# A state-space convolution with a SwiGLU layer: the powers of the large lag factor from TensorE and PSUM

## The chip, the core and the metric

The kernel runs on one core of a Trainium2 chip. The core has five engines that each work off a queue of their own in order: TensorE (PE in the profile; its weight loads are shown apart as PEld), VectorE (DVE), ScalarE (ACT), GpSimd (POOL) and SyncE (SP), which here only issues DMAs. They wait for each other by semaphores. The metric is the device time of one execution in microseconds.

## What is computed

Two layers, each a state-space convolution with a residual, followed by a SwiGLU feed-forward part with a residual, over 2048 positions of 512 channels. Both layers use the same parameters, so the filter K is formed once. Cut to what matters:

```python
def _A_ref(u, A_re, A_im, B_re, B_im, C_re, C_im, log_dt, Dskip):
    dt = jnp.exp(log_dt)[:, None]
    logdA = dt * (A_re + 1j * A_im)                        # [512, 128]
    dB = dt * (B_re + 1j * B_im)
    P = jnp.exp(logdA[:, :, None] * l[None, None, :])      # l = 0 .. 2047
    K = jnp.einsum("dn,dnl,dn->dl", C_re + 1j * C_im, P, dB).real
    y = irfft(rfft(u, 2 * L) * rfft(K, 2 * L))[:L]         # per channel
    return y + u * Dskip

def _B_ref(x, w_gate, w_up, w_down):
    return (silu(x @ w_gate) * (x @ w_up)) @ w_down

x = A_u
for _ in range(2):
    x = x + _A_ref(layernorm(x), ...)
    x = x + _B_ref(layernorm(x), ...)
```

## The kernel before

The first 290 us form the filter. The 512 channels go in eight chunks of 64 channels; the 128 states lie on the partitions. A lag is split as l = 32 a + z, with a from 0 to 63 and z from 0 to 31. For each chunk the kernel forms a large factor, the powers exp(32 a r) times a sine or cosine (tiles `re` and `im`, 64 channels by 65 values of a), and a small factor `g` with the weights in it (64 channels by 32 values of z). `r` is the real rate `rho` = dt A_re. For each channel TensorE multiplies both over the states (`lags`, 128 products of 32 by 64 into the PSUM tile `pk`). ScalarE copies `pk` out (`ks`, L476), TensorE spreads it (`spread`, `kp`), ScalarE copies that (`kt`, L947), and `spectra` turns it into the filter's spectrum with matrices of cosines, for four residues q in turn: products `pw` (L507), a copy by ScalarE (L516), sums by GpSimd (L518 to L528), and stores of `wdr` by SP.

The magnitudes of the large factor are formed by `gen_exp`, on ScalarE alone. `mz` holds six small powers (L393). `re[:, :, a]` for a from 1 to 32 and `mu[:, :, a - 32]` for a from 33 to 63 hold exp(32 a r): an exponential of 128x64 (L398) for each odd a and each a that divides by 8, and the others as squares of those at half the exponent (L401). That makes 39 exponentials and 4 squarings for a chunk.

The three engines ACT, DVE and PE have an order written out by hand in this stage (`manual_schedule`); the rows of SP and GpSimd, and all that follows the stage, are placed by a scheduler. The hand-written order is a loop of seven turns over i:

- `lags(i)`, the rest of the third and the whole fourth spectrum of chunk i-1, `spread_in` (the copy `ks`)
- on VectorE the small factor of chunk i+1 (`gen_g`) and its large one (`gen_e`), and the phases of chunk i+2 (`gen_turns`, `gen_reduce`)
- on ScalarE the sines of chunk i+2 (`gen_trig`), then `kt`, then `gen_exp` of chunk i+2, whose pieces `take(ex, n)` are laid between copies of spectra and other work
- two times in a turn `norm_units(3, 9)`: three tiles of the feed-forward weights are loaded (`st`), squared by ScalarE (`sq`, L309), and multiplied by ones on TensorE (`nrm`, L313), for bounds on the weights' norms. The second half of this, `norm_units(0, 0)`, gives the products to TensorE. In the second one of a turn they stand between the second and the third spectrum, so TensorE's queue stops there until the squares are done.
- one unit of `second`, a part of the input's forward transform (`pf`, L279)

[...] Two tiles of two banks each (tag `big`) serve `pk` and `kp` by turns; four tiles of one bank (tag `sml`) serve the spectra, the norms and `pf`.

The feed-forward stage from about 300 us on takes most of the time and is one long run of fp16 products on TensorE.

Of the kernel before, what the change touches and what calls it, by code (L numbers as in the profile page):

```python
# [22 lines left out]
P = 128  # L23
# [4 lines left out]
HD = D // 2  # L28
# [6 lines left out]
DC = 64  # L35
NCH = D // DC
ZP = (1, 2, 3, 4, 8, 16)
NZ = len(ZP)
NA = NZ + 16
# [7 lines left out]
def dft_constants():  # L47


    j = np.arange(P)[:, None]  # L50
    r = np.arange(P)[None, :]
    ef = np.zeros((P, 4, 3, P), np.float64)
    ei = np.zeros((P, 4, 3, P), np.float64)
    ek = np.zeros((P, 4, 3, 2, P), np.float64)
    for q in range(4):
        f = q + 8 * r + 0.5
        e = np.exp(-2j * np.pi * ((j * f) / 1024.0))
        ef[:, q, 0], ef[:, q, 1], ef[:, q, 2] = e.real, e.imag, -e.real
        et = e.T / 512.0
        ei[:, q, 0], ei[:, q, 1], ei[:, q, 2] = et.real, et.imag, -et.imag  # L60
        for c in range(1, 4):
            ec = np.exp(-2j * np.pi * (((j + P * c) * f) / 1024.0))
            ek[:, q, c - 1, 0], ek[:, q, c - 1, 1] = ec.real, ec.imag
    am = np.zeros((P, NA), np.float64)
    am[:, :NZ] = ZP
    am[:, NZ:] = 32.0 * np.arange(17, 33)
    halves = []
    for e in (ef * 256.0, ei * 8192.0):
        hi = e.astype(np.float16)
        halves.append(np.stack([hi, (e - hi).astype(np.float16)], 3))  # L70
    return [a.astype(np.float32) for a in (ef, ei, ek, am)] + halves
# [3 lines left out]
def kernel(ctx, tc, x, a_re, a_im, b_re, b_im, c_re, c_im, log_dt, d_skip,  # L75
                           w_gate, w_up, w_down, c_ef, c_ei, c_ek, c_am, c_eh, c_eih, out):
    nc = tc.nc
    V, A, G, PE = nc.vector, nc.scalar, nc.gpsimd, nc.tensor
# [29 lines left out]
    nc.sync.dma_start(am, c_am)  # L108
    xne = tl([P, 2, 4, D], "xne", "gb")
    xe, ne = xne[:, 0], xne[:, 1]  # L110
    for c in range(0, 4, 2):
# [18 lines left out]
    wx = sb.tile([P, D], F16, name="wx")  # L130
# [203 lines left out]

    mz2 = tl([P, 2, NZ, DC], "mz2", "y1")
    tmp = btl[:, :4 * HD].rearrange("p (i s d) -> p i s d", i=2, s=8), tl([P, 16, DC], "tmp", "t")

    def gen_tiles(ch):  # L340
# [47 lines left out]
    def gen_exp(ch, ts):  # L388

        re, im, mu, xz, mz, t16 = ts  # L390
        r_ = rho[:, ch * DC:(ch + 1) * DC]
        for lv, m in enumerate(ZP):
            A.activation(mz[:, lv], r_, AF.Exp, scale=float(m))  # L393
            yield
        G.memset(re[:, :, 0], 1.0)
        for a0, o in ((0, re), (32, mu)):
            for a in [a for a in range(a0 + 1, a0 + 33) if a < 64 and (a % 2 or a % 8 == 0)]:
                A.activation(o[:, :, a - a0], r_, AF.Exp, scale=32.0 * a)  # L398
                yield
            for st in (2, 4):  # L400
                A.activation(o[:, :, st:33:2 * st] if a0 == 0 else o[:, :, st::2 * st],  # L401
                             re[:, :, (a0 + st) // 2:(a0 + 34) // 2:st], AF.Square)
                yield

    def gen_e(ts):
# [57 lines left out]
    def lags(ts, g):  # L463
        re, im = ts[:2]
        pk = pbig([P, 16, 64], "pk")
        for d in range(DC):
            grp, dd = d % 4, d // 4
            d = 16 * grp + dd
            o = pk[32 * grp:32 * grp + 32, dd, :]
            PE.matmul(o, lhsT=g[:, 0, :, d], rhs=re[:, d, 0:64], start=True, stop=False, tile_position=(0, 32 * grp))  # L470
            PE.matmul(o, lhsT=g[:, 1, :, d], rhs=im[:, d, 0:64], start=False, stop=True, tile_position=(0, 32 * grp))
        return pk

    def spread_in(pk):
        ks = tl([P, 4, 16, 16], "ks", "nn")
        A.activation(ks, pk.rearrange("p d (c a) -> p a c d", a=4), AF.Copy)  # L476
        return ks
# [78 lines left out]
    def take(it, n):  # L556
        for _ in range(n):
            next(it, None)
# [287 lines left out]
    ts = [None] * (NCH + 2)  # L846
# [13 lines left out]
    with tc.manual_schedule(engines={mybir.EngineType.Activation, mybir.EngineType.DVE, mybir.EngineType.PE}):  # L860
        ts[0], ts[1] = gen_tiles(0), gen_tiles(1)
        ex = gen_exp(0, ts[0])
# [42 lines left out]
        ex = gen_exp(1, ts[1])  # L905
# [2 lines left out]
        take(ex, 13)  # L908
        take(fw[7], 1)
        kt2 = tl([P, 2, 4, 16, 16], "kt2", "xf")  # L910
        sec = [(h, q) for h in range(2) for q in QORD]
        sp = iter(())
        for i in range(NCH - 1):
            pk = lags(ts[i], gs[i])
            more = i + 2 < NCH
            tn = rd = f = iter(())
            if more:
                ts[i + 2] = gen_tiles(i + 2)
                tn = gen_turns(i + 2, ts[i + 2])
            gs[i + 1] = tl([P, 2, 32, DC], "g", ("gb", "ga")[i % 2])  # L920
            gg, ge = gen_g(i + 1, ts[i + 1], gs[i + 1]), gen_e(ts[i + 1])
            take(ex, 100)
            take(sp, 2)
            norm_units(3, 9)
            norm_units(0, 0)
            ks = spread_in(pk)
            for g in (gg, tn, gg, tn):
                take(g, 1)
            if more:
                rd = gen_reduce(ts[i + 2])  # L930
                next(rd)
            for g in (gg, gg, ge, gg, ge, gg, gg, rd, rd, ge, rd, rd, ge, rd, rd, rd, rd):
                take(g, 1)
            while tops:
                tops.pop(0)()
            take(sp, 1)
            take(gg, 2)
            kp = spread(i, ks)
            if more:
                f = second(*sec[i])  # L940
                next(f)
            take(gg, 2)
            if more:
                tr = gen_trig(ts[i + 2])
                take(tr, 1)
            kt = kt2[:, i % 2]
            A.activation(kt, kp, AF.Copy)  # L947
            take(tr, 1)
            take(f, 1)
            take(tr, 1)  # L950
            if more:
                sp = spectra(i, kt, 0, NB)
                take(sp, 1)
                ex = gen_exp(i + 2, ts[i + 2])
                take(ex, 10)
                norm_units(3, 9)
                take(ex, 4)
                take(sp, 2)
                norm_units(0, 0)
                take(ex, 14)  # L960
                take(sp, 2)
                sizes(i, kt, ks)
                take(ge, 4)
                take(gg, 1)
                while tops:
                    tops.pop(0)()
                ts[i] = gs[i] = None
            else:
                sizes(i, kt, ks)
                take(ge, 4)  # L970
                take(gg, 1)
# [19 lines left out]
        i = NCH - 1  # L991
# [99 lines left out]
```

## Time and profile before

| what | value |
|---|---|
| median of three runs | 1200.64 us (1198.14 to 1202.4) |
| the profiled execution | 1200.92 us, its span 1199.1 us |
| PE busy, share of the span | 1102.7 us, 92% |
| PEld | 857.4 us, 72% |
| DVE | 1022.5 us, 85% |
| ACT | 650.4 us, 54% |
| POOL | 176.4 us, 15% |

Shares over the whole span say little about the stage that is changed. In the page's forty slices of 30 us, ACT has a 9 or an 8 in the tenths place from the second to the ninth slice, that is up to 270 us, and then falls off; DVE and PE are busy in most slices. What follows is read from windows and timelines of that stage. In a row of a timeline stand the start and the length in microseconds, the engine, the line, the operation, what it writes and reads, the shapes, how many instructions the row joins, and in brackets the idle time ahead of it and what ended it. Rows that join many instructions give the time that they took together.

### The profile page before, as it was taken

How to read it: one execution, taken by the hardware profiler on the slowest of the kernel's cores; microseconds unless marked ns; L12 is line 12 of the kernel's file. 1: busy time of each engine (PE TensorE's matmuls, PEld its weight loads, DVE VectorE, ACT ScalarE, POOL GpSimd, SP SyncE). 2: the span in 40 equal slices, each digit the busy share in tenths (PEclk: the TensorE clock that was granted, in tenths of full speed). 3: DMA queues.
4: the chain of work that ended last, by engine and by line, in shares of the span. 5: the costliest groups of instructions: out<-in, count | busy, mean ns of one | idle time of the engine just before them, and what ended most of it. 6: DMA issues, size and time to landing. Idle time of an engine off the chain costs nothing.

```text
span 1199.1 us, 25374 instructions
## 1 busy us (share of the span) xinstructions
PE 1102.7 (92%) x10220; PEld 857.4 (72%) x10220; DVE 1022.5 (85%) x1621; ACT 650.4 (54%) x1400; POOL 176.4 (15%) x225
## 2 busy tenths in 40 slices
PE   2978998988988989999999999999999989999998
PEld 2846776766875767778777686868687776867875
DVE  7988999996979998999999999999993899983211
ACT  6999999982256544636654533745432552224111
POOL 1104355542310010001100100110000010000000
PEclk9979899989999999999999999999999999999999
DMA  6444455558389428332344354334434144311000
GB/s 228 124 110 116 108 124 117 124 149 238 113 288 238 127 71 205 126 120 89 93 135 135 115 163 143 111 96 138 142 125 137 45 106 131 122 53 45 15 24 18
DMA packets 137161, 147.05 MB, mean 123 GB/s; under 512 B 76177, under 2 KB 85393, under 8 KB 137042
## 3 DMA queue, kind: packets, MB, share of 16 engines
q1 hardware_dynamic: 132178, 128.64, 35.8%
q0 software_dynamic: 4864, 16.78, 5.9%
q8 instruction: 80, 1.31, 0.5%
q14 instruction: 39, 0.32, 0.1%
HBM read 98.71 MB, written 28.31 MB: 106 GB/s over the span
## 4 chain that ended last, share of the span: by engine, by line
PE 46%; DVE 17%; issue 4%; DMA 3%; ACT 2%; POOL 1%; SPq 1%; DVEq 0%; ACTq 0%; POOLq 0%
PE pgu L821 8%; PE pgu L822 8%; PE pgu L823 8%; PE py L835 5%; PE py L837 5%; PE py L836 5%; PE pi L716 4%; PE pf L263 4%; DVE t L697 2%; DVE yk L700 2%; DVE yk L697 2%; DVE z L219 2%; DMA mix<-nn 1%; DVE sg L827 1%; DVE bt L219 1%
## 5 line engine op out<-in xcount | busy, mean ns | idle before, releaser
L821 PE MATMUL pgu<-mix,wsl 128*128 128x256 f16 x1280 | 349.8, 273 | 5.6 <-DVE sg L827 4.1
L823 PE MATMUL pgu<-mix,wsl 128*128 128x256 f16 x1280 | 349.7, 273 | 1.5 <-DVE wsl L593 1.5
L822 PE MATMUL pgu<-mix,wsl 128*128 128x256 f16 x1280 | 349.8, 273 | 0.0
L835 PE MATMUL py<-wsl,hh 128*128 128x512 f16 (+1 forms) x352 | 134.5, 382 | 11.0 <-DVE xg L840 4.9
L822 PEld LDWEIGHTS <-wsl 128*128 128x128 f16 x1280 | 125.5, 98 | 22.3 <-issue 6.6
L823 PEld LDWEIGHTS <-wsl 128*128 128x128 f16 x1280 | 125.6, 98 | 16.7 <-DVE wsl L593 1.8
L837 PE MATMUL py<-wsl,hl 128*128 128x512 f16 (+1 forms) x352 | 134.8, 383 | 2.7 <-DVE hl L829 2.7
L821 PEld LDWEIGHTS <-wsl 128*128 128x128 f16 x1280 | 125.6, 98 | 16.0 <-issue 0.3
L697 DVE TENSOR_TENSOR t<-uu,w 128x1024 f32<-128x1024 f32 x96 | 117.4, 1223 | 5.9 <-DMA uu<-udr 5.6
L836 PE MATMUL py<-wsl,hh 128*128 128x512 f16 x320 | 122.3, 382 | 0.0
L826 ACT ACTIVATE sg<-pgu,sc 128x512 f32<-128x512 f32 x80 | 54.5, 681 | 117.5 <-PE pgu L823 99.7
L700 DVE TENSOR_TENSOR yk<-yk,t 128x1024 f32<-128x1024 f32 x96 | 117.4, 1222 | 0.1
L827 DVE SCALAR_TENSOR_TENSOR sg<-pgu,sc,sg 128x512 f32<-128x512 f32 x80 | 60.0, 750 | 49.6 <-ACT sg L826 49.5
L507 PE MATMUL pw<-kt,ek 128*128 128x256 f32 (+2 forms) x420 | 102.0, 382 | 0.0
L716 PE MATMUL pi<-yl,mix 128*128 128x256 f16 x672 | 91.7, 273 | 6.3 <-ACT yl L705 4.4
L828 ACT ACTIVATE hh<-sg 128x512 f16<-128x512 f32 x80 | 50.1, 626 | 78.0 <-DVE sg L827 77.9
L507 PEld LDWEIGHTS pw<-kt,ek 128*128 128x128 f32 x420 | 81.5, 202 | 10.9
L263 PE MATMUL pf<-z,eh 128*128 128x256 f16 x576 | 75.8, 273 | 0.0
L716 PEld LDWEIGHTS <-mix 128*128 128x128 f16 x672 | 65.2, 98 | 12.3 <-issue 2.2
L705 ACT ACTIVATE yl<-mix,sy 128x512 f16<-128x512 f32 x56 | 40.2, 718 | 61.1 <-DVE mix L702 60.7
L214 POOL TENSOR_TENSOR rs<-mv,mhalf 128x2 f32<-128x2 f32 (+1 forms) x21 | 35.2, 1675 | 246.7 <-ACT mv L213 246.7
L836 PEld LDWEIGHTS <-hh 128*128 128x128 f16 (+1 forms) x352 | 34.7, 99 | 48.4 <-issue 13.5
(231 smaller groups left out, 2285.0 us busy)
## 6 DMA issues: line engine op xcount, KB each, us to landing
w<-wdr SPq DMA_DIRECT2D x96, 256.0 KB, 2.7
uu<-udr SPq DMA_DIRECT2D x96, 256.0 KB, 3.0
udr<-u POOLq DMA_DIRECT2D x32, 256.0 KB, 2.4
wdr<-wo SPq DMA_DIRECT2D x96, 64.0 KB, 2.4
udr<-u SPq DMA_DIRECT2D x16, 256.0 KB, 2.8
g<-tmp POOLq DMA_DIRECT2D x8, 512.0 KB, 4.6
g<-btl POOLq DMA_DIRECT2D x8, 512.0 KB, 5.9
n<-ndr SPq DMA_DIRECT2D x16, 256.0 KB, 3.0
```

The costliest lines, as they stand in the source:

```text
L263: PE.matmul(pf[:, o], lhsT=e, rhs=m, start=k == 0, stop=k == len(terms) - 1)
L507: PE.matmul(pw[:, i], lhsT=e, rhs=kt[:, :, c + 4 * k0:4 * k1:4, :].rearrange("p g k d -> p k g d"), start=c == 0, stop=c == 3)
L697: V.tensor_tensor(t, uu.unsqueeze(1).to_broadcast([P, 2, 2, HD]), w.unsqueeze(2).to_broadcast([P, 2, 2, HD]), OP.mult)
L700: V.tensor_tensor(yk, yk, t, OP.add)
L716: PE.matmul(pi[:, o], lhsT=e, rhs=m, start=k == 0, stop=k == len(terms) - 1)
L821: PE.matmul(o, lhsT=wgu(wi, k, 0)[:, fs], rhs=nh[:, k], start=k == 0, stop=False)
L822: PE.matmul(o, lhsT=wgu(wi, k, 0)[:, fs], rhs=nlo[:, k], start=False, stop=False)
L823: PE.matmul(o, lhsT=wgu(wi, k, 1)[:, fs], rhs=nh[:, k], start=False, stop=k == 3)
L827: V.scalar_tensor_tensor(sg, pgu[:, 1], sc6[:, 4:5], sg, OP.mult, OP.mult)
L835: PE.matmul(py[:, r], lhsT=hh[:n, f, rc], rhs=wd(f, 0)[:n], start=f == 0, stop=False)
L836: PE.matmul(py[:, r], lhsT=hh[:n, f, rc], rhs=wd(f, 1)[:n], start=False, stop=False)
L837: PE.matmul(py[:, r], lhsT=hl[:n, f, rc], rhs=wd(f, 0)[:n], start=False, stop=f == FT - 1)
```

## The change

From the third chunk on (chunk 2) `gen_exp` returns after the six small powers. The exponents 32 a r of the large factor are then formed by TensorE. GpSimd splits the rates of two chunks into three bf16 parts that add up to the fp32 value (`parts`). A DMA transpose (`turned`) turns each chunk's parts, so that 112 partitions hold, for two groups of 16 channels, the parts by channel, with the states along the free axis (`lts`). A constant table holds the multiples 32 a in blocks, zero elsewhere. It is appended to the constant `c_am`, bf16 values packed in pairs as fp32 words, and loaded once into the second half of `kt2` (`tab`). A product of both gives 16 channels by 32 exponents in one bank; two of them fill a tile `pm` of the `big` tag, and one exponential of 128x32x32 reads it and writes a half of `re` or `mu` (`gen_mags`). A chunk takes four such steps: eight products of 512 columns and four exponentials. `kt` now uses one buffer for all chunks. The place for the parts is in the tile of `mz`, the remainders are kept in `wx`, which is used later for weights, and `lts` in the last part of `btl`.

```diff
+    tab = np.zeros((2, 4, 16, 2, 2, 16, 32), np.float32)
+    for e in range(2):
+        for d in range(16):
+            tab[e, :3, d, 0, e, d] = 32.0 * np.arange(1, 33)
+            tab[e, :3, d, 1, e, d] = 32.0 * np.arange(33, 65)
+    tab = (tab.reshape(P, -1).view(np.uint32) >> 16).astype(np.uint16).view(np.float32)
+    am = np.concatenate([am.astype(np.float32), tab], 1)
...
-    mz2 = tl([P, 2, NZ, DC], "mz2", "y1")
+    mzp = tl([P, 4 * HD], "mzp", "y1")
+    mz2 = mzp[:, :2 * NZ * DC].rearrange("p (c l d) -> p c l d", c=2, l=NZ)
+    pt = mzp[:, 3 * HD:].bitcast(BF16).rearrange("p (c g q d) -> p c g q d", c=2, g=4, q=4)
+    r1 = wx.bitcast(F32)[:, :2 * DC].rearrange("p (c g d) -> p c g d", c=2, g=4)
+    lts = btl[:, 6 * HD:].bitcast(BF16).rearrange("p (c g n) -> p c g n", c=2, g=2)
+    G.memset(pt, 0.0)
...
         G.memset(re[:, :, 0], 1.0)
+        if ch > 1:
+            return
...
+    def parts(ch):
+        src = rho[:, ch * DC:(ch + 2) * DC].rearrange("p (c g d) -> p c g d", c=2, d=16)
+        hi, mid, lo = (pt[:, :, :, q] for q in range(3))
+        G.tensor_copy(hi, src)
+        G.tensor_tensor(r1, src, hi, OP.subtract)
+        G.tensor_copy(mid, r1)
+        G.tensor_tensor(lo, r1, mid, OP.subtract)
+
+    def turned():
+        for c in range(2):
+            nc.sync.dma_start_transpose(lts[:, c], pt[:, c].rearrange("p g q d -> p (g q d)"))
+
+    def gen_mags(ch, ts):
+        for k, o in enumerate((ts[0][:, :, 1:33], ts[2][:, :, 1:])):
+            for h in range(2):
+                pm = pbig([P, 32, 32], "pm")
+                for e in range(2):
+                    PE.matmul(pm[:, 16 * e:16 * e + 16], lhsT=lts[:112, ch % 2, h], rhs=tab[:112, k, e],
+                              start=True, stop=True)
+                yield
+                A.activation(o[:, 32 * h:32 * h + 32], pm[:, :, :32 - k], AF.Exp)
                 yield
...
         kt2 = tl([P, 2, 4, 16, 16], "kt2", "xf")
+        kta = kt2[:, 1].rearrange("p k a d -> p (k a d)")
+        nc.sync.dma_start(kta, c_am[:, NA:])
+        tab = kta.bitcast(BF16).rearrange("p (k e d a) -> p k e d a", k=2, e=2, d=16)
+        parts(2)
+        turned()
+        mags = None
...
         for i in range(NCH - 1):
+            if mags:
+                take(mags, 1)
             pk = lags(ts[i], gs[i])
...
             take(ex, 100)
+            if mags:
+                take(mags, 2)
             take(sp, 2)
...
             ks = spread_in(pk)
+            if mags:
+                take(mags, 1)
+            if i % 2 == 0 and 0 < i < NCH - 2:
+                parts(i + 2)
+                turned()
...
-            kt = kt2[:, i % 2]
+            kt = kt2[:, 0]
...
                 ex = gen_exp(i + 2, ts[i + 2])
-                take(ex, 10)
+                take(ex, 100)
+                mags = gen_mags(i + 2, ts[i + 2])
+                take(mags, 2)
                 norm_units(3, 9)
-                take(ex, 4)
                 take(sp, 2)
                 norm_units(0, 0)
-                take(ex, 14)
+                take(mags, 2)
                 take(sp, 2)
```

The order of the rows on two engines, in turn 2. The first place is ScalarE from the six small powers (`mz`, now in the tile `mzp`) to the first copy of a spectrum and on (`s`); `sq` are the squares. Before:

```order
L393 ACTIVATE mz_154<-rho 128x64 x6
L398 ACTIVATE re<-rho 128x64 x4
L309 ACTIVATE sq<-st 128x344 x3
L398 ACTIVATE re<-rho 128x64 x4
L516 ACTIVATE s_1558<-pw 128x512
L398 ACTIVATE re<-rho 128x64 x12
L401 ACTIVATE re<-re 128x64x8
L401 ACTIVATE re<-re 128x64x4
L516 ACTIVATE s_1593<-pw 128x512
```

and now:

```order
L405 ACTIVATE mzp<-rho 128x64 x6
L441 ACTIVATE re<-pm 128x32x32
L316 ACTIVATE sq<-st 128x344 x3
L555 ACTIVATE s_1514<-pw 128x512
L441 ACTIVATE re<-pm 128x32x32
L555 ACTIVATE s_1539<-pw 128x512
```

One large exponential stands where four small ones stood ahead of the squares, and one where sixteen small ones and two squarings stood behind them.

The second place is ScalarE at the end of that turn and the start of the next, around the copy `ks` of the lag products; `xr<-xi` is the first step of the next phases. Before:

```order
L537 ACTIVATE ks,wsum<-kt_478 128x1024
L398 ACTIVATE mu<-rho 128x64 x19
L401 ACTIVATE mu<-re 128x512
L401 ACTIVATE mu<-re 128x256
L516 ACTIVATE s_1772<-pw 128x512
L309 ACTIVATE sq<-st 128x344 x3
L476 ACTIVATE ks<-pk 128x1024
L364 ACTIVATE xr<-xi 128x384
```

and now:

```order
L576 ACTIVATE ks,wsum<-kt_479 128x1024
L441 ACTIVATE mu<-pm 128x32x31
L555 ACTIVATE s_1704<-pw 128x512
L316 ACTIVATE sq<-st 128x344 x3
L515 ACTIVATE ks<-pk 128x1024
L441 ACTIVATE mu<-pm 128x32x31
L376 ACTIVATE xr<-xi 128x384
```

The 21 rows of `mu` behind the sum `ks,wsum` have become one, and a second one now stands behind the copy `ks` and ahead of the next phases.

The third place is TensorE from the last product of the norms to the first lag product `pk`; `pw` is the third spectrum. Before:

```order
L313 MATMUL nrm<-sq,onesb 128x344
L507 MATMUL pw<-kt_478,ef 128x256
L507 MATMUL pw<-kt_478,ek_84 128x256 x3
L507 MATMUL pw<-kt_478,ef 128x256
L507 MATMUL pw<-kt_478,ek_84 128x256 x3
L470 MATMUL pk<-re,g 32x64
```

and now, from behind the same product to ahead of the first `pk` (`btl` holds the turned parts, and `kt_479` the table):

```order
L438 LDWEIGHTS btl
L438 MATMUL pm<-kt_479,btl 128x512
L438 LDWEIGHTS btl
L438 MATMUL pm<-kt_479,btl 128x512
L546 MATMUL pw<-kt_479,ef 128x256
L546 MATMUL pw<-kt_479,ek_84 128x256 x3
L546 MATMUL pw<-kt_479,ef 128x256
L546 MATMUL pw<-kt_479,ek_84 128x256 x3
L438 LDWEIGHTS btl
L438 MATMUL pm<-kt_479,btl 128x512
L438 LDWEIGHTS btl
L438 MATMUL pm<-kt_479,btl 128x512
```

A pair of products stands on either side of the third spectrum; a third pair stands between the first and the second spectrum, and the fourth directly behind the lag products. On GpSimd the first two sets of `parts` stand before and behind the statistics of the first norm (L204 to L207), and the third in turn 2 behind the sums of the third spectrum.

More of the change, by code (lines that the diff above doesn't have):

```diff
@@ L107 @@
     am = sb.tile([P, NA], F32, name="am")
-    nc.sync.dma_start(am, c_am)
+    nc.sync.dma_start(am, c_am[:, :NA])
     xne = tl([P, 2, 4, D], "xne", "gb")
@@ L402, in gen_exp @@
                              re[:, :, (a0 + st) // 2:(a0 + 34) // 2:st], AF.Square)
+                yield
[16 more added lines that the diff above has]
+                              start=True, stop=True)
+                yield
+                A.activation(o[:, 32 * h:32 * h + 32], pm[:, :, :32 - k], AF.Exp)
                 yield
```

## The prediction

> **What bounds the kernel now.** The diff touches only the stage that forms the filter, the first 290 us, so I began with windows of that stage. In turn i of its loop ScalarE forms the magnitudes of chunk i+2, so turns 0 to 5 hold every edit. I cut the windows where ScalarE starts the copy `ks` (L476), which frees the result of the lag products (the last three columns are TensorE clock, DMA share, GB/s):
>
> ```profile
> 68.68:101.25 32.57, 30.25 (x378) 22.19 (x377) 29.42 (x38) 31.71 (x83) 10.19 (x11) 0.84 0.47 118
> 101.25:133.92 32.67, 27.36 (x372) 20.30 (x371) 30.62 (x39) 32.06 (x83) 10.15 (x17) 0.90 0.50 119
> 133.92:165.33 31.41, 28.91 (x394) 23.20 (x395) 29.41 (x36) 31.27 (x83) 15.07 (x16) 1.00 0.47 114
> 165.33:196.78 31.45, 26.69 (x375) 20.65 (x375) 30.90 (x40) 31.31 (x83) 16.22 (x17) 0.95 0.50 119
> 196.78:228.09 31.31, 28.54 (x386) 22.59 (x386) 31.09 (x40) 31.17 (x83) 16.62 (x17) 0.95 0.52 120
> 228.09:260.22 32.13, 28.01 (x378) 21.34 (x377) 31.93 (x42) 31.69 (x83) 12.68 (x17) 0.89 0.56 135
> ```
>
> Columns are the length, then busy time of PE, PEld, DVE, ACT and POOL. ACT is full, but DVE is within 0.2 to 3 us of it. So ACT time saved is worth 8.2 us at most (191.54 us of turns less 183.36 us of DVE work). Whether even that comes depends on where in the turn it is saved. The timeline of ACT in turn 3:
>
> ```profile
> 165.33 1.00 ACT L476 ACTIVATE ks<-pk 128x1024 f32<-128x1024 f32 x1
> 166.23 0.51 ACT L364 ACTIVATE xr<-xi 128x384 int32<-128x384 f32 x1
> ...
> 182.93 0.74 ACT L398 ACTIVATE re<-rho 128x64 f32<-128x64 f32 x4
> 183.51 1.23 ACT L309 ACTIVATE sq<-st 128x344 bf16<-128x344 f32 x3
> 184.65 0.74 ACT L398 ACTIVATE re<-rho 128x64 f32<-128x64 f32 x4
> ...
> 190.75 3.16 ACT L398 ACTIVATE mu<-rho 128x64 f32<-128x64 f32 x19
> 193.66 1.65 ACT L401 ACTIVATE mu<-re 128x512 f32<-128x512 f32 x2
> ...
> 196.78 1.00 ACT L476 ACTIVATE ks<-pk 128x1024 f32<-128x1024 f32 x1
> ```
>
> and of TensorE in the same turn:
>
> ```profile
> 173.82 0.70 PE L507 MATMUL pw<-kt,ef 128*128 128x256 f32 x2 [0.41 <-ACT kt L947]
> ...
> 184.04 1.18 PE L313 MATMUL nrm<-sq,onesb 128*128 128x344 bf16 x3 [3.04 <-ACT sq L309]
> 185.02 1.06 PE L507 MATMUL pw<-kt,ef 128*128 128x256 f32 x2
> 185.87 2.65 PE L507 MATMUL pw<-kt,ek 128*128 128x256 f32 x6
> ...
> 195.85 0.70 PE L507 MATMUL pw<-kt,ef 128*128 128x256 f32 x2
> ```
>
> These show a second ring. TensorE waits for the squares of L309, forms the third spectrum and the lag products, which end where L507 goes on at 195.85. L476 needs those products. From L476 to the end of the squares ACT takes 19.4 us (165.33 to 184.74); from there to the end of the lag products TensorE takes 11.1 us. Together 30.5 of 31.45 us: TensorE comes 0.9 us before ACT has worked off its exponentials. Turns 2, 4 and 5, by the same two places:
>
> ```profile
> 152.05 1.24 ACT L309 ACTIVATE sq<-st 128x344 bf16<-128x344 f32 x3
> 152.58 1.07 PE L313 MATMUL nrm<-sq,onesb 128*128 128x344 bf16 x3 [1.20 <-ACT sq L309]
> 162.69 0.70 PE L507 MATMUL pw<-kt,ef 128*128 128x256 f32 x2
> ...
> 214.92 1.23 ACT L309 ACTIVATE sq<-st 128x344 bf16<-128x344 f32 x3
> 215.45 1.20 PE L313 MATMUL nrm<-sq,onesb 128*128 128x344 bf16 x3 [1.97 <-ACT sq L309]
> 226.53 0.70 PE L507 MATMUL pw<-kt,ef 128*128 128x256 f32 x2
> ...
> 246.25 1.23 ACT L309 ACTIVATE sq<-st 128x344 bf16<-128x344 f32 x3
> 260.05 0.70 PE L507 MATMUL pw<-kt,ef 128*128 128x256 f32 x2
> ```
>
> Squares to lag end is 9.4, 10.4 and 12.6 us. The granted clock makes the difference (windows of 1 us; columns as above):
>
> ```profile
> 154.00:155.00 1.00, 1.00 (x7) 0.87 (x6) 1.00 (x2) 1.00 (x7) 0.57 (x1) 1.00 1.23 164
> 216.00:217.00 1.00, 1.00 (x4) 0.69 (x3) 1.00 (x2) 1.00 (x6) 0.00 (x0) 0.50 1.06 193
> 250.00:251.00 1.00, 1.00 (x4) 0.77 (x3) 1.00 (x2) 1.00 (x4) 0.70 (x1) 0.50 0.72 248
> ```
>
> After a pause of 1.20 us in turn 2 it stayed at 1.00, after 1.97 us in turn 4 it fell to 0.50, and in turn 5 it was still 0.50 at 250.
>
> **The change part by part.**
> *ACT.* Per turn 39 exponentials and 4 squarings go: in the rows above those of L398 and L401, and more of them in the gap between. From 184.65 to 196.78, 12.1 us, ACT does little else, so some 8 to 9 us. Four exponentials of 128x1024 from PSUM come. No such exponential is in the trace; the nearest row is L476, the same shape from PSUM, 0.90 us to the next start. I take 0.95 each, with 0.9 and 1.2 as bounds. ACT's own work falls by some 5 us. But almost all of that lies behind the squares. Ahead of them stand now the first new exponential in place of four small ones (+0.35) and the fourth one, right behind L476 (+0.95): the way from L476 to the squares' end grows by 1.3 us, to 20.7.
>
> *TensorE.* Eight bf16 products of 512 columns per turn. The same shape, back to back:
>
> ```profile
> 102.01 0.81 PE L313 MATMUL nrm<-sq,onesb 128*128 128x512 bf16 x3
> 102.75 0.64 PE L486 MATMUL kp<-ks,ident 128*32 128x256 f32 x8
> ```
>
> 0.74 us for three, 0.25 each. Four of them stand between squares and lag end: +1.0 us. The other four fill pauses: the pair before the second spectrum lies in the wait for the squares. Shorter at half cost or longer at a clock of 0.50, the four are worth 0.8 to 2.0.
>
> *The new ring.* 19.4 + 1.3 + squares to lag end + 1.0 + 0.1, an estimate, for the handover. With turn 2's 9.4 that is 31.2 us a turn, with turn 4's 10.4 it is 32.2. Which one holds depends on the pause ahead of L313. In turn 3 TensorE took 18.3 us from the lag end to the end of the second spectrum (162.69, with 3.04 us of pause before 184.04), 0.4 of it waiting for `kt`, which then comes in time since TensorE is later by a pair; with two more pairs that is 18.9 us. The first square is done 17.6 + 0.95 + 0.95 + 0.45 = 19.95 us after L476. The pause is about 1.1 us, beside the 1.20 that kept the clock and below the 1.97 that lost it; the norms that follow are sparse too. I take the half clock in two of turns 1 to 5.
> At full clock turns 1 to 5 give 31.5 (turn 1's squares are larger) and four times 31.2, 156.3 against 158.97 in the windows: -2.7; each halved turn adds 1.0. So -0.7, with -2.7 and +2.3 as bounds. In turn 0 only +0.35 on ACT and +1.0 on TensorE stand in the ring, whose TensorE part had 2.8 us to spare (lag end 98.45, L476 at 101.25):
>
> ```profile
> 98.45 0.70 PE L507 MATMUL pw<-kt,ef 128*128 128x256 f32 x2
> ```
>
> So -1.4 there, and -2.1 for the loop.
>
> *GpSimd.* Three sets of four operations on 128x128 that read and write SBUF. The order puts two sets beside the first norms' statistics, before 32 us, while DVE works without a gap and ACT comes to wait for it. What such work costs DVE, and that wait:
>
> ```profile
> 128.56 1.21 DVE L411 TENSOR_TENSOR im<-im,re 128x1024 f32<-128x1024 f32 x1
> 161.62 1.40 POOL L524 TENSOR_TENSOR wo<-s 128x192 f32<-128x192 f32 x2
> 162.48 1.62 DVE L411 TENSOR_TENSOR im<-im,re 128x1024 f32<-128x1024 f32 x1
> 51.28 1.12 ACT L383 ACTIVATE re<-im 128x1024 f32<-128x1024 f32 x1 [1.05 <-DVE im L376]
> ```
>
> At most 0.41 us for each of eight, 3.3; at least nothing. Turn 3 had six more GpSimd operations than turn 0 and 1.5 us more DVE time, 0.25 each; not all of the eight meet such a DVE instruction, so I take +1.2. [...] The third set falls into turn 2, where DVE has 0.3 us left beside the new ring: at most 0.5, in the range.
>
> *DMA.* Six transposes and one load of the table join SP's queue; the load has some 30 us until the first use, and the memset of the parts comes before any work of GpSimd that is waited for. A transpose of `nn` landed in 2.7 us:
>
> ```profile
> mix<-nn SPq DMA_TRANSPOSE x60, 2.7
> ```
>
> After each stand only stores of `wdr`, and the weights are used a turn (31 us) later: nothing. If that cover were gone, 2.7 us for a chunk's first pair. One `kt` buffer in place of two costs nothing: its readers end with the fourth spectrum, before `kp`. The third set waits for a transpose on GpSimd; behind it stand a copy and the second accumulating DMA, some 9 us later in the turn: nothing, or 1 to 2 us once.
>
> *After the loop* nothing is changed, but the scheduler sets some of the feed-forward stage in another order. TensorE is busy there nearly all the time:
>
> ```profile
> sum 899.00, PE 861.13 PEld 668.64 DVE 752.42 ACT 392.28 POOL 70.85; mean PE 95.68 PEld 74.29 DVE 83.60 ACT 43.59 POOL 7.87
> ```
>
> 38 us of its 899 are idle; I count the reordering as zero, plus or minus 3. An earlier loop end reaches the end whole: TensorE's work from there on is the same.
>
> Sum: 1200.92 - 2.1 + 1.2 = 1200.0 in the terms of the profiled execution, which lies 0.28 above the median of 1200.64. **Forecast 1199.7**, own range 1197 to 1203.5.
>
> **The rivals.**
> *The clock holds* in all five turns: -2.7 - 1.4 + 1.2, **1197.7**. For it speaks turn 2, against it turns 3 to 5. [...]
> *DVE is the only bound*: if the squares do not hold TensorE up, ACT's 5 us a turn are free and each turn shrinks to its DVE time, -8.2 + 1.2, **1193.4**. For it speaks that DVE is full; against it the wait of L313 in all of these turns, which stands ahead of the work that was taken out.
> *The long half clock, slower*: as in turn 5, where squares to lag end took 12.6 us. Five such turns are 3.2 us each above the full clock, +16.0 on -2.9: **1213.7**; two or three give 1205 to 1207. It decides once the pause and the sparse norms together pass about 2 us. For it speaks turn 5 (2.49 us of wait, 0.50 still at 250); against it the shorter pause.
> *GpSimd holds up the first statistics* and with them DVE, where its copies find DVE at work. Two in a row that wait like this one, handed on whole, are +8.4, **1208.1**; for it speaks that DVE has no gap there, against it that this copy was the exception beside the 1.40 us of two L524 above.
>
> ```profile
> 154.43 4.17 POOL L518 COPY w0r<-s 128x128 f32<-128x128 f32 x1 [2.63 <-ACT s L516]
> ```
>
> *The change does not act*: the reordered tail decides, **1200.6** plus or minus 3 or more.
>
> **How the numbers follow.** Forecast 0.45, clock holds 0.20, DVE alone 0.12, long half clock 0.10, GpSimd 0.06, no effect 0.07. About 0.3% (3.6 us) is what a measurement of this kernel can tell from no change: 1197.0 to 1204.2. Faster: a tenth of the forecast, 0.4 of the second, 0.85 of the third, 0.3 of the last: 0.25. Slower: 0.9 of the fourth, most of the GpSimd case, small parts of the forecast and of the last: 0.19. Same: 0.56. For 8 in 10 the range reaches from the DVE case, 1194, to two or three long half clocks and the GpSimd case, 1208.
>
> **What would show it.** Right: ACT no longer full, with idle time ahead of `ks` L515 that a lag product ends; L320 still waiting for squares, by about 1 us; turns of 31.2 or 32.2 us, the longer ones with 0.50 in the clock; first turn about 31.2. Wrong: turns at DVE's length with DVE full (DVE alone); half clocks of 7 us; DVE idle before 30 us behind L204 to L207; or new exponentials far from 0.95 us or pairs far from 0.5 us. The sum falls if TensorE meets the squares without a wait, for then ACT's time behind them counts.

## The result, and the profile after

The changed kernel takes **1189.98 us** (median of 7 runs, 1187.41 to 1194.84), the kernel before 1200.82 us (7 runs, 1196.75 to 1202.4): ratio 0.992, 95% interval 0.9895 to 0.9946. In a second series of runs it was 1196.05 us (6 runs, 1188.35 to 1199.28) against 1201.11: ratio 0.9932, 0.9901 to 0.9963. The mean of these 13 runs, 1192.6 us, is what the experiments are compared with; the kernel before has 1200.9. So the change gains 8 us, and 1199.7 with a range from 1194 was too high. The second series by itself lies inside that range; the first, and the mean of both, lie under it.

The profiled run took 1194.56 us (span 1192.8, clock 0.983; the 13 runs have 0.980 to 0.989). Its turns, cut where ScalarE starts `ks` (now L515); the columns are length, busy time of PE, PEld, DVE, ACT and POOL, then TensorE clock, DMA share and GB/s. The last row is turn 6, which forms no exponentials:

```profile
68.65:98.88 30.23, 27.39 (x373) 19.72 (x372) 28.21 (x36) 25.72 (x43) 11.63 (x10) 0.89 0.47 123
98.88:130.27 31.39, 28.37 (x391) 21.75 (x390) 30.46 (x38) 26.46 (x43) 13.65 (x19) 1.00 0.56 132
130.27:161.30 31.03, 28.07 (x391) 21.79 (x390) 30.75 (x39) 26.14 (x43) 16.43 (x18) 1.00 0.47 114
161.30:193.96 32.66, 29.75 (x391) 23.08 (x390) 32.52 (x40) 26.20 (x44) 16.09 (x20) 0.95 0.56 138
193.96:225.38 31.42, 28.11 (x391) 21.89 (x390) 30.84 (x40) 26.14 (x43) 12.41 (x17) 1.00 0.47 108
225.38:256.34 30.96, 28.17 (x391) 21.84 (x390) 30.79 (x40) 26.20 (x43) 11.26 (x16) 1.00 0.57 142
256.34:282.50 26.16, 23.18 (x370) 18.29 (x368) 25.48 (x37) 7.89 (x13) 12.84 (x13) 1.00 0.78 204
```

ScalarE is no longer full, 26 of 31 us. The timeline of ScalarE and TensorE in turn 2 shows where the 5 us went:

```profile
148.70 1.02 ACT L441 ACTIVATE re<-pm 128x1024 f32<-128x1024 f32 x1
149.62 1.23 ACT L316 ACTIVATE sq<-st 128x344 bf16<-128x344 f32 x3
...
155.57 1.03 ACT L441 ACTIVATE mu<-pm 128x992 f32<-128x992 f32 x1 [1.33 <-PE pm L438]
156.48 0.60 ACT L555 ACTIVATE s<-pw 128x512 f32<-128x512 f32 x1
156.95 1.25 ACT L316 ACTIVATE sq<-st 128x344 bf16<-128x344 f32 x3
161.30 1.02 ACT L515 ACTIVATE ks<-pk 128x1024 f32<-128x1024 f32 x1 [3.11 <-PE pk L510]
```

```profile
150.14 1.07 PE L320 MATMUL nrm<-sq,onesb 128*128 128x344 bf16 x3 [1.63 <-ACT sq L316]
151.05 0.59 PE L438 MATMUL pm<-kt,btl 112*128 112x512 bf16 x2
```

ScalarE now waits 3.11 us for the lag products ahead of `ks`, as the ring of the prediction has it; TensorE still waits for the squares, by 1.63 us. A new exponential takes 0.92 us to the next start (148.70 to 149.62), a pair 0.43. Turns 0 to 5 sum to 187.69 us against 191.54 here; but in the profile of the second series they sum to 192.0: two of turns 1 to 5 fell to half clock there and one here, and turn 0 held 9.2 us of it in place of 6.8. One profile of each kernel can't settle a difference of 4 us in the loop.

Turn 6, at 1.00 clock in both, went from 28.71 to 26.16 us. In the kernel before:

```profile
260.22:288.93 28.71, 23.02 (x368) 18.28 (x369) 25.35 (x34) 7.01 (x12) 14.39 (x16) 1.00 0.76 201
```

```profile
265.41 0.40 SPq L979 DMA_DIRECT2D mix<-in_c_ei_dram  x1
265.86 0.42 SPq L630 DMA_DIRECT2D mix<-udr  x1
...
269.80 0.56 SPq L307 DMA_DIRECT2D st<-in_B_w_up_dram  x1
...
278.14 0.49 ACT L309 ACTIVATE sq<-st 128x344 bf16<-128x344 f32 x1 [7.63 <-DMA st<-in_B_w_up_dram]
...
278.68 0.31 PE L313 MATMUL nrm<-sq,onesb 128*128 128x344 bf16 x1 [2.82 <-ACT sq L309]
```

These rows are from the timelines of SyncE, ScalarE and TensorE. SyncE had issued two loads of `mix`, 768 and 1024 KB, 4 us ahead of the weights; the weights landed 8.3 us after their issue, and TensorE lost 2.82 us. In the changed kernel the same two loads are issued 8 us ahead of the weights, which land 2.5 us after their issue:

```profile
258.38 0.40 SPq L1034 DMA_DIRECT2D mix<-in_c_ei_dram  x1
258.84 0.42 SPq L669 DMA_DIRECT2D mix<-udr  x1
264.29 2.24 SPq L569 DMA_DIRECT2D wdr<-wo  x3
266.63 0.55 SPq L314 DMA_DIRECT2D st<-in_B_w_up_dram  x1
...
272.60 0.31 PE L320 MATMUL nrm<-sq,onesb 128*128 128x344 bf16 x1 [0.29 <-ACT sq L316]
```

GpSimd's first sets lie where the prediction feared them, and nothing came of it: turn 0 begins at 68.65 us (68.68 before).

```profile
11.06 0.60 POOL L423 CAST mzp<-rho 128x128 bf16<-128x128 f32 x1 [8.51 <-DVE rho L904]
...
15.18 0.41 POOL L204 TENSOR_SCALAR rs<-mv 128x4 f32<-128x4 f32 x1 [1.05 <-DVE mv L203]
```

Behind the last lag products (windows from the last `ks` to the end, columns as above) the two kernels look alike:

```profile
288.93:1199.10 910.17, 872.20 (x7185) 676.72 (x7185) 755.32 (x1246) 396.68 (x746) 70.85 (x91) 0.99 0.39 118
```

```profile
282.50:1192.80 910.30, 875.29 (x7185) 678.34 (x7185) 758.50 (x1249) 395.84 (x746) 74.95 (x93) 0.99 0.38 118
```

They are not: the trace's clock records hold 13.7 us at half clock in this stage before, and 23.9 us after. TensorE is busy for 96% of this stage, so as an estimate a stretch at half clock costs half its length; without that the stage took 903.4 and 898.4 us. The order of this stage, which the scheduler chooses, is another one. The second profile of the changed kernel agrees (911.6 us with 23.9 at half clock: 899.7).

### The profile page after: what moved, and what is told of

It reads as the page before. It is cut to its first block, busy times and chain, and to the rows that moved or that the text cites. A ratio compares the mean times of both kernels' runs of the same rounds, so it can differ in the third digit from the quotient of the medians.

```text
span 1192.8 us, 25266 instructions
## 1 busy us (share of the span) xinstructions
PE 1108.3 (93%) x10268; PEld 861.2 (72%) x10268; DVE 1026.5 (86%) x1621; ACT 618.0 (52%) x1166; POOL 185.0 (16%) x238
## 4 chain that ended last, share of the span: by engine, by line
PE 35%; DVE 26%; issue 5%; ACT 3%; DMA 2%; POOL 2%; SPq 1%; DVEq 0%; ACTq 0%; POOLq 0%
PE pgu L860 6%; PE pgu L861 6%; PE pgu L862 6%; DVE t L736 4%; PE py L874 4%; PE py L875 4%; PE py L876 3%; DVE yk L739 3%; DVE yk L736 3%; PE pi L755 3%; PE pf L270 2%; DVE z L226 2%; DVE sg L866 2%; POOL rs L221 2%; DVE bt L226 1%
## 5 line engine op out<-in xcount | busy, mean ns | idle before, releaser
L546 PE MATMUL pw<-kt,ek 128*128 128x256 f32 (+2 forms) x420 | 98.6, 373 | 0.0
L546 PEld LDWEIGHTS pw<-kt,ek 128*128 128x128 f32 x420 | 78.7, 195 | 9.5
L221 POOL TENSOR_TENSOR rs<-mv,mhalf 128x2 f32<-128x2 f32 (+1 forms) x21 | 38.3, 1824 | 263.2 <-ACT mv L220 255.8
L736 DVE TENSOR_TENSOR yk<-u,w0r 128x1024 f32<-128x1024 f32 x56 | 68.2, 1218 | 0.3 <-ACT u L272 0.3
```

Of the source, the lines that this page charges most:

```text
L546: PE.matmul(pw[:, i], lhsT=e, rhs=kt[:, :, c + 4 * k0:4 * k1:4, :].rearrange("p g k d -> p k g d"), start=c == 0, stop=c == 3)
L736: V.tensor_tensor(t, uu.unsqueeze(1).to_broadcast([P, 2, 2, HD]), w.unsqueeze(2).to_broadcast([P, 2, 2, HD]), OP.mult)
```

## The experiments

Theories at the start: **ring** (ScalarE up to the squares, then TensorE up to the lag products, sets the turn) against **VectorE alone**. A time is the median of 4 to 12 runs where nothing else is said; the kernel before had medians of 1199.6 to 1201.2 us beside them.

**The same kernel again.**

> The changed kernel unchanged, for a second profile. If the loop decides: last lag products about 282.5 us after the start as in the first profile (288.9 in the kernel before), and 910 us from there to the end. If the difference between the profiled pair (-6.4 us) and the medians (-10.8 us) lies in the granted clock, then a run near 1190 us shows fewer half clocks than the first profile (0.983) in the feed-forward stage and the same loop.

1196.05 us; last lag products at 285.9 us, 911.6 from there. Turns 1 to 5 were 33.33, 30.82, 31.89, 32.81 and 31.25 us; 33.33 and 32.81 are those with a half clock of 3.4 us. The feed-forward stage had as many half clocks as in the first profile, so what a run near 1190 looks like isn't shown; over the 13 runs time falls as the mean clock rises (1188.35 us at 0.987, 1199.28 at 0.980).

**One exponential twice.**

```diff
                 A.activation(o[:, 32 * h:32 * h + 32], pm[:, :, :32 - k], AF.Exp)
+                if k == 0 and h == 0:
+                    A.activation(o[:, 32 * h:32 * h + 32], pm[:, :, :32 - k], AF.Exp)
```

> Changed kernel with the first new exponential of each chunk done twice (the second writes the same values), ahead of the squares. Theory 'ring' (the turn is set by ScalarE up to the squares, then TensorE up to the lag products): each of six turns grows by the 0.92 us of one exponential, +5.5 us, more by 1 us for each turn whose longer pause (1.6 + 0.9 us) halves the clock: 1195 to 1201 us. Rival 'VectorE alone': ScalarE has 3 us to spare in each turn, so 0, 1190 us.

1215.0 us, far over either. Turns 1 to 5 took 33.9 to 34.3 us, each with one half clock of 3.4 us. The pause ahead of the products grew to 2.73 us, and the clock followed. Windows of TensorE in turn 2, cut on the grid on which the clock's records change (length, busy time, clock, DMA share, GB/s):

```profile
152.98:156.39 3.41, 1.00 (x5) 1.00 1.06 202
156.39:159.80 3.41, 3.41 (x10) 0.50 0.80 201
159.80:163.22 3.42, 3.42 (x70) 1.00 0.00 0
```

So 0.92 us of ScalarE and 1.7 us of lost TensorE time (an estimate, half of the 3.41 us at 0.50) make the 2.6 us a turn: the ring holds, 'VectorE alone' falls. Two more costs came along: turn 6 waited for its weights as in the kernel before (29.7 us), and the feed-forward stage stood in a third order.

**More work for VectorE.**

```diff
         V.tensor_tensor(g[:, 0, 16:], g[:, 0, :16], zr, OP.mult)
+        if ch > 1:
+            V.tensor_tensor(g[:, 0, 16:], g[:, 0, :16], zr, OP.mult)
```

> Changed kernel with one product of 128x1024 on VectorE (1.22 us) done twice in each of turns 1 to 6. Theory 'ring' with VectorE just behind it: the turns have 0.9, 0.3, 0.1 and up to 0.5 us of VectorE to spare and turn 6 has 10, so about 0.3 to 1.1 us in each of turns 1 to 5, +3.5 us, 1193 to 1195. Rival 'VectorE alone': 1.22 in each of turns 1 to 5, +6.1, 1196. If VectorE is not near the limit at all: 0.

1213.22 us: turns 2 to 5 took 36.3 to 37.0 us. Neither theory has that. The edit moved GpSimd: in four turns the scheduler put the second accumulating DMA of `g` behind a copy and two products instead of ahead of them, and the lag products waited 4.1 to 4.5 us for it in three of them. GpSimd in turn 2 (its timeline):

```profile
154.88 3.04 POOL L565 TENSOR_TENSOR wo<-s 128x192 f32<-128x192 f32 x2
157.86 0.87 POOL L501 DMA_DIRECT2D g<-btl  x1
```

In the changed kernel this DMA is issued at 148.86 us. The run says nothing on VectorE; it shows what a new place in GpSimd's queue is worth.

**Products behind the next lag products.**

```diff
             pk = lags(ts[i], gs[i])
+            if mags:
+                norm_units(0, 0)
...
                 take(sp, 2)
-                norm_units(0, 0)
                 take(mags, 2)
```

> Changed kernel with the three squared-weight products at the end of a turn moved behind the next lag products, so that TensorE does not wait for the squares there. Theory 'ring': the pause of 1.6 us goes and the turn falls to VectorE's own time, 30.5 us or so in place of 31.0 to 32.7: -1.5 to -3 us, 1187 to 1188.5. Rival 'VectorE alone': no change, 1190. In both the clock should stay at 1.00 through all turns.

1201.84 us, a miss on both sides. The wait moved: the next three squares found their buffers still held by the late products (`sq` waited 18.0 us in three turns for them), and the lag products waited up to 2.8 us for `g`.

**All of the change but the exponentials; fill for the pauses.** `no_mags` gives `gen_exp` its old steps back and drops `gen_mags`. The fill is this, ahead of the products that wait for squares at a turn's end:

```diff
+    def fill(n):
+        pm = pbig([P, 32, 32], "pm")
+        for e in range(2 * n):
+            PE.matmul(pm[:, 16 * (e % 2):16 * (e % 2) + 16], lhsT=lts[:112, 0, 0], rhs=tab[:112, 0, e % 2],
+                      start=True, stop=True)
...
                 take(sp, 2)
+                fill(3)
                 norm_units(0, 0)
```

What was expected of `no_mags`, and then of three kernels with fill, `no_mags_fill`, `after_fill` and `early_pair_fill`:

> The kernel before with everything of the change except the new exponentials: the parts on GpSimd, the transposes, the load of the table and the single kt buffer stay, but ScalarE forms the magnitudes as before. Theory A (the gain comes from the new exponentials): time and loop as in the kernel before, 1201 us, last lag products at 288 to 289 us; GpSimd's early sets cost 0. Rival B (the gain comes from what lies around them, the other order of the feed-forward stage above all): 1192 to 1196 us.

> The same, with three pairs of 512-column products, whose result nobody reads, ahead of the three products that wait for the squares at the end of each turn. Theory 'share of a window' (the clock falls to 0.50 for 3.4 us whenever TensorE is busy for less than about 0.45 of one 3.41 us stretch of a fixed grid): the half clocks of turns 1 to 5 go (20 us of them in the first profile of before), the clock in turns 1 to 5 is 1.00, and these turns end at ScalarE's own 31.3 us, so -2 us against the run without the fill, 1199. Rival 'the pause itself' (clock unaffected): 0.

> The changed kernel with the same three pairs ahead of the products that wait for the squares at the end of each turn; they take 1.3 us, less than the pause of 1.65 us. Theory 'share of a window': no half clock in turns 1 to 5 (one or two of 3.4 us in the two profiles so far), the turns all at 31.0 us, -1.7 us for each that goes: 1189 to 1191 us, and less spread between runs. Rival: the pairs only add work: 1192 to 1195.

> The changed kernel with the second pair of each turn moved ahead of the products that wait for the squares, two pairs of fill behind it, and in turn 0 eight pairs of fill ahead of the lag products and five ahead of the first products that wait for squares. Theory 'ring plus clock': the ring is 0.43 us shorter in each of five turns, down to VectorE's 30.7 us, -1.5 us; no half clock between 50 and 290 us (13.6 to 23.8 us so far), of which about half is on the way: -3 us more; 1187 to 1189 us. Rival 'VectorE and its transfers alone': turns unchanged, 1192 us.

`no_mags` 1199.74 us (ratio 1.0005, 0.9979 to 1.003): the parts, transposes, table and `kt` buffer cost or give nothing that shows (the interval reaches from -2.5 to +3.6 us). The fill did part of what it should in the loop: with it the clock of turns 1 to 5 was 1.00 in both changed kernels (in `no_mags_fill` two half clocks stayed), and the last lag products stood at 285.4 us (`no_mags_fill`, 287.2 without), 282.7 (`after_fill`) and 281.8 (`early_pair_fill`). The turns didn't all come down to 31.0 us: at full clock turns 1 to 5 still took up to 31.8 us in `after_fill` and 32.9 in `early_pair_fill`. Yet the times were **1203.31, 1198.67 and 1197.96 us**, 4 us over `no_mags` and 5 to 6 over the changed kernel. It arose behind the loop, in 915.3, 914.6 and 911.4 us. In these three, in `double_exp` and in `late_products` the scheduler gave the feed-forward stage one and the same order, which neither the kernel before nor the changed one has. Of the 16 groups of down projections (tile `py`), the distances between the starts of the 6th, 7th, 8th and 9th (us) show the orders; two kernels a row, in the sequence of their names:

```
before, no_mags                52.2 59.6 58.6    52.1 59.7 60.5
after, after_again             56.3 58.1 53.7    56.4 58.1 53.6
after_fill, no_mags_fill       57.6 59.7 54.2    57.6 59.7 54.8
```

That made the order a theory of its own: call these orders B, A and C.

**The loop alone.** Both kernels cut off behind the last `ks`, which is stored, and two variants of the changed one; `loop_dve` does this:

```diff
-        V.tensor_tensor(xz[1], am[:, :NZ].unsqueeze(2).to_broadcast([P, NZ, DC]), t_.unsqueeze(1).to_broadcast([P, NZ, DC]), OP.mult)
+        for _ in range(1 + (ch > 1)):
+            V.tensor_tensor(xz[1], am[:, :NZ].unsqueeze(2).to_broadcast([P, NZ, DC]), t_.unsqueeze(1).to_broadcast([P, NZ, DC]), OP.mult)
```

What was expected of `loop_before`, `loop_after`, `loop_fill` and `loop_dve`:

> The kernel before, cut off behind the copy of the eighth chunk's lag products; everything behind the loop (the last spectra, the state-space outputs and the feed-forward stage) is left out. The profile of the whole kernel has that copy end at 290.0 us, and a store follows: about 294 us.

> The changed kernel cut off at the same place, with the same parts left out. Against the cut kernel before: if the whole gain of 8 us lies in the loop, -8. If the loop gives what the profiles show (-6.4 and -3.0 us at the last lag products) and the rest comes from the order and the clock of the feed-forward stage: -3 to -6. In turn 6 the square waits for its weights in the kernel before and not here: -2.6 of it.

> The changed kernel with the early second pair and the fill of TensorE's pauses (as in early_pair_fill), cut off at the same place, with the same parts left out. Theory 'ring plus clock': -2 to -4 against the cut changed kernel, with a clock of 1.00 from 80 us on. Rival 'VectorE and its transfers alone': 0 to -1, from turn 0.

> The changed kernel with one product of 128x384 on VectorE (0.55 us) done twice in each of turns 0 to 5, at a place that leaves GpSimd's order as it is, cut off at the same place, with the same parts left out. 'VectorE's ring ties with the other one': +0.3 to 0.5 us a turn in turns 1 to 5, +1.5 to 2.5 us against the cut changed kernel. 'ScalarE and TensorE alone set the turn': under +1.

In this sequence they took 291.29, **292.0**, 288.19 and 291.92 us (4 or 5 runs each, spread 2 to 3 us). The cut kernel before loses only 0.28 us to the squares in turn 6 (25.8 us long); of the two loads of `mix` it still issues the one of 768 KB, but not the one of 1024 KB. Without that wait the loops are level (in the means the changed one is 0.6 us slower, plus or minus 1.1), though the clock rose from 0.943 to 0.967 in the profiles. `loop_fill` is 3.8 us faster in the medians (3.1 plus or minus 1.5 in the means), as 'ring plus clock' has it; the run doesn't separate the fill from the moved pair, and its profile, that of the slowest run, still has one half clock in turns 3 and 4. `loop_dve` shows no cost (means 0.6 us apart, plus or minus 1.0): 0.55 us of VectorE a turn still find room, or nearly.

**The order against the exponentials.** `before_order` is the kernel before with one move, by which the scheduler happens to choose order A; `early_pair` and `early_pair_start` keep order A as well.

```diff
         take(sp, 2)
-        norm_units(0, 0)
         take(sp, 3)
...
         pk = lags(ts[i], gs[i])
+        norm_units(0, 0)
```

The second edit is that of `early_pair`, the third what `early_pair_start` adds (`fill` as above):

```diff
                 take(sp, 2)
+                take(mags, 1)
                 norm_units(0, 0)
-                take(mags, 2)
+                take(mags, 1)
```

```diff
+            if i == 0:
+                fill(8)
             pk = lags(ts[i], gs[i])
...
             norm_units(3, 9)
+            if i == 0:
+                fill(5)
             norm_units(0, 0)
```

What was expected of `before_order`, `early_pair` and `early_pair_start`:

> The kernel before, with its exponentials, and one move: the last products of squares in turn 6 stand behind the lag products, so that these do not wait for the late weights; by that move the scheduler gives the feed-forward stage the order that it has in the changed kernel. Theory 'order and turn 6': -2.6 us in turn 6 and -4 us in the feed-forward stage, 1193 to 1195 us with no new exponential at all. Rival 'the exponentials and the clock': turn 6 alone, 1198; with the order worth nothing.

> The changed kernel with the second pair of each turn ahead of the products that wait for the squares; the feed-forward stage keeps the changed kernel's order. Theory 'ring': 0.43 us less in each of five turns where VectorE leaves room, -1 to -2 us: 1190.5 to 1192 against 1192.6 (mean of the changed kernel's 13 runs). Rival 'VectorE's ring ties': 0.

> As early_pair, and in turn 0 eight pairs of fill ahead of the lag products and five ahead of the first products that wait for squares; the feed-forward stage keeps the changed kernel's order. Theory 'clock': the half clocks around 57 to 74 us (13.6 us of them) go, of which TensorE's ring gets back 1 to 2 us in turn 0: 1189 to 1191, the fastest so far. Rival: the fill only adds work ahead of the first lag products: 1192 to 1194.

Last, `other_order`, a fourth order:

```diff
-BOOST = 1 << 20
+BOOST = 300
```

> The changed kernel with the same instructions, and a smaller head start for the urgent work of the feed-forward stage in the scheduler's priorities (300 in place of 1048576): the loop is the same to the instruction, the feed-forward stage stands in a fourth order. If the order is worth several us by itself, the time moves by 3 us or more in either direction, all of it behind the last lag products; if not, 1192.6 within 1 us.

`before_order` **1194.66 us** (12 runs; ratio 0.9947, 0.9926 to 0.9967) without a single new exponential: 6 of the 8 us. Its three distances are 56.2, 58.2 and 54.0 us, and behind the loop TensorE has the changed kernel's sequence of products.

`early_pair` 1192.47: no gain that shows. The pause falls to 1.2 us as it should, but two turns fell to half clock, in another the lag products waited 1.18 us for an exponential (`mu`), and in a fourth 0.66 us for the DMA of `g`: a third ring, from VectorE over GpSimd's DMA, follows closely. `early_pair_start` 1191.99, level with the changed kernel at a clock of 0.992 against 0.985; in three turns of its profile the lag products wait 0.3 to 0.7 us for `g`. Against `early_pair_fill` it lacks two pairs of fill a turn and has order A in place of C; their loops end at 281.66 and 281.83 us, and the rest is

```profile
281.66:1188.30 906.64, 870.40 (x7185) 676.04 (x7185) 758.60 (x1250) 396.28 (x746) 72.88 (x92) 0.99 0.39 118
```

```profile
281.83:1193.20 911.37, 873.49 (x7185) 677.18 (x7185) 759.40 (x1250) 396.42 (x746) 71.96 (x91) 0.99 0.39 118
```

By the estimate above 1.7 of these 4.7 us are half clock (13.7 and 17.1 us), and 3 go with the order. `other_order` 1193.87 us (1191.18 to 1195.78): a fourth order, and no difference that shows. Orders needn't differ in time; A and C do. What it is in order C that costs the time stays open.

**The exponentials in one order.** A pair with the move of `before_order` and order A in both, that differs in the exponentials alone.

What was expected of `same_order_old_exp`, with the old exponentials, and of `same_order_new_exp`:

> Everything of the change but the new exponentials (as no_mags), with the last products of squares in turn 6 behind the lag products and the feed-forward stage in the changed kernel's order. As before_order: 1194 to 1196 us.

> The changed kernel with the same move, in the same order. If the exponentials are worth what the first forecast of the loop said (-2.1 us): 1192 to 1194, about 2 us under its partner. If the cut loops are right: level with it or up to 1 us over.

They took 1194.09 us (8 runs, mean 1194.6) and 1193.53 us (6 runs, mean 1192.6): -0.6 in the medians, -2.0 in the means, plus or minus 2.4. With `before_order` on the one side and the 13 runs of the changed kernel on the other (20 against 19 runs) the means differ by **-2.1 plus or minus 1.9 us**; that pool mixes series taken apart from each other, and its 13 runs lack the move.

`no_mags` and `same_order_old_exp` differ in the move alone: 1199.74 and 1194.09 us, timed apart from each other, with the kernel before at 1201.21 and 1200.31 us beside them. In their profiles (1199.34 and 1196.92 us) the last `ks` starts at the same time, and what differs lies behind it, as it does in part for `before_order` (third row; the kernel before took 910.17):

```profile
287.17:1197.50 910.33, 873.98 (x7185) 677.39 (x7185) 755.59 (x1246) 396.39 (x746) 70.05 (x91) 0.99 0.39 118
287.14:1195.10 907.96, 871.44 (x7184) 676.66 (x7182) 761.20 (x1260) 396.58 (x747) 75.57 (x99) 0.99 0.40 118
285.64:1193.10 907.46, 870.91 (x7183) 676.45 (x7181) 761.65 (x1260) 396.67 (x747) 75.05 (x99) 0.99 0.39 118
```

## Why the forecast missed

- **Loop, -2.1 us: borne out in cause; the size is open.** ScalarE's 5 us a turn became a wait of 3.1 us for the lag products and waits for the pairs, as forecast, and the turns at full clock took 31.0 to 31.4 us where 31.2 was forecast. What the exponentials are worth by themselves is -2.1 plus or minus 1.9 us over the kernels with order A, and about nothing in the cut loops; between the two it stays open.
- **Inside that term:** an exponential was taken at 0.95 us and measured 0.92; a pair at 0.5, 0.43. The half clock was taken at +1.0 a turn and is 1.7; it was expected in two of five turns and came in one (first profile) and two (second). The pause is 1.6 to 1.7 us, not 1.1.
- **GpSimd, +1.2 us: wrong.** Beside the first two sets VectorE lost 0.4 us in all against the kernel before: a product of 128x384 from two tiles (`xi`) took 0.78 us in place of 0.55, and two scalings of 128x512 (`xne`, by per-partition values) took 0.65 in place of 0.54. Even that didn't arrive: turn 0 begins where it began. `no_mags`, with all of GpSimd's sets, is level with the kernel before. Which of VectorE's instructions such work lengthens was not shown: another product from two tiles beside the first set (`t`, 128x1024) took 1.22 us, and 1.23 before.
- **"I count the reordering as zero, plus or minus 3", after the loop: the step that failed.** Turn 6 and what follows it, counted as nothing, gave 6 of the 8 us, as `before_order` and the step from `no_mags` to `same_order_old_exp` show. Two parts of it are seen in profiles: TensorE's wait for late weights in turn 6 (2.82 us down to 0.29), which the sum left out since it stopped at turn 5; and the scheduler's order, B before and A after: by the estimate above the stage without its half clocks took 903.4 and 901.8 us in the two profiles with B, 896.5 to 901.4 in the eight with A, and 902.8 to 906.8 in the five with C. How the 6 us divide between the two was not separated: the one move that takes the wait away changes the order too. The profiles lean to the order: `no_mags` waits only 0.77 us for the squares in turn 6, and is no faster than the kernel before. But behind the loop they show 2 to 3 of the 6 us; where the rest lies, one profile of each doesn't tell.
- **Spread, and no term:** the 2.7 us by which the first series' median lies under the mean of both.
- **"The clock holds", 1197.7:** half right. It holds in most turns, and the mean clock rose from 0.979 to 0.985. But a clock that the fill raised to 0.988 and 0.990 bought nothing where order C came with it.
- **"DVE is the only bound", 1193.4** (its own terms add up to 1193.6), was near the time by luck: `double_exp` and `loop_dve` both speak against it.
- **"The long half clock", 1213.7,** didn't come: in turns 1 to 5 of both profiles each half clock lasted 3.4 us, not 7. (Two or three such turns add up to 1204.1 and 1207.3 in its terms, not 1205 to 1207.)
- **"An earlier loop end reaches the end whole"** doesn't hold where the order changes: `no_mags_fill` and `early_pair_fill` ended the loop earlier than `no_mags` and the changed kernel, and took 3.6 and 5.4 us longer.

## What to carry over

Where a scheduler orders the stage behind an edit, compare that order before trusting a sum of a few us, and try the order by itself: here one move that leaves the work as it is gave the larger part of the gain. Count a changed stage to its last turn, with the loads that its queues issue late. And where an engine is relieved, look for the next ring through the old wait: here ScalarE had 5 us less to do in a turn, and turn 2 became 0.4 us shorter (31.41 to 31.03).

## What the runs showed of the hardware

**In these profiles the half clock followed TensorE's busy share in single stretches of a grid of 3.41 us.** The grid is that of the clock's records. In the 20 profiles, of the stretches at full clock (from 45 us on), those followed by one at 0.50 were:

```
busy share of the stretch   followed by half clock
under 0.40                  101 of 101
0.40 to 0.50                 37 of 81
0.50 to 0.60                  8 of 104
0.60 and more                 0 of 5154
```

Moving the edges of the stretches by 0.02 us shifts these counts by a few.

Two neighbours from the changed kernel, turn 2 and turn 3, with pauses of 1.63 and 1.72 us (columns as in `double_exp`):

```profile
148.72:152.14 3.42, 1.85 (x9) 1.00 1.02 191
152.14:155.55 3.41, 3.41 (x20) 1.00 0.98 223
179.44:182.86 3.42, 1.55 (x8) 1.00 1.03 186
182.86:186.27 3.41, 3.41 (x10) 0.50 1.01 207
```

1.85 us busy kept the clock, 1.55 lost it. Whether a pause of 1.7 us costs 1.7 us more thus hangs on where the grid cuts it, which differs from run to run (an edge lies at 184.86 us in the profile before, at 182.86 in this one); that fits the spread of 1187 to 1199 us of one kernel.

**A place in GpSimd's queue cost more than the work.** In `extra_dve` 1.22 us more on VectorE moved one accumulating DMA behind a copy and two products, and turns 2, 4 and 5 grew by 5.5 to 6 us, half clocks included.
